# Two layers of cached attention and FFN for one token: w_down's rows and a head's keys laid adjacent per partition

## The chip, the cores and the metric

The kernel runs on one core of a Trainium2 chip. The metric is the device time of one execution in microseconds; the number for a kernel is the median over its runs. A profiled execution of its own gives the page and the trace; it has its own time and its own span (from the first to the last instruction).

## The reference

Four sequences (B = 4) each bring one token of 512 values. Two layers are run, and both use the same weights and the same caches, so every key and value is needed twice.

```
def attention(x):                       # Hq = 32 heads, Hkv = 8, Sk = 4096, Dh = 128
    q = x @ wq                          # [4, 512] @ [512, 4096]
    k, v = k_cache, v_cache             # [4, 8, 4096, 128] bf16, one kv head for 4 q heads
    p = softmax(q . k * Dh ** -0.5)
    return (p . v) @ wo                 # [4, 4096] @ [4096, 512]

def ffn(x):                             # F = 1792
    return (gelu(x @ w_gate) * (x @ w_up)) @ w_down

for layer in (1, 2):
    x = x + attention(layernorm(x))
    x = x + ffn(layernorm(x))
```

Keys and values are 33.5 MB each; w_gate, w_up and w_down are 1.8 MB each. The order in which the 4096 keys of a head are gone through doesn't matter, as long as keys and values use the same one. The same holds for the 1792 columns between w_gate, w_up and w_down.

## The kernel before

The partitions of SBUF are P = 128. A head's 4096 keys are split into NT = 2 tiles of 2048; a tile holds CH = 16 keys in each partition, 4 KB, and is loaded by one DMA of 512 KB (`cache_tile`; `load_pairs` loads the tiles of two heads by one DMA of 1 MB; `pump_head` loads both tiles of one head by one DMA of 1 MB, three times, for the last values). Before the change tile t of a head is its keys 2048 t to 2048 t + 2047, and partition p of it holds 16 neighbouring keys, so the whole tile is one stretch of 512 KB in memory.

All loads go through SP's queue (`dq`), in the order in which the code issues them; SP waits where the buffer of a load is still in use. Keys have one set of buffers (`KP`, 8 heads by 2 tiles). Values have a ring of eight buffers (`V_SLOTS`), which `VRing.pump` fills whenever one comes free.

The work goes sequence by sequence. The first layer's attention of sequence 0 runs alone (`attend_first`), and then, for each b:

- `dense(b, ...)`: the first layer's FFN of sequence b.
- the second layer's queries for b, its scores on the keys that lie in SBUF, and its values;
- `attend(b + 1, ...)`: as soon as the second layer's scores of b have read a key buffer, the keys of sequence b + 1 are loaded into it, turned in place on VectorE (`Keys.turn`, L484) and used for the first layer. Values of both are taken from the ring by `Values.step` and `Streamed.fill`.

After b = 3 (`attend_last`), `dense_last` computes the second layer's FFN for all four sequences at once.

The FFN is written in two ways. `ffn_in` (L374) has the weights as the stationary operand: for each of KF = 14 blocks c of 128 columns, and each of KD = 4 blocks k of 512 inputs, 128 x 128 weights are loaded and 32 columns are streamed past them: 56 weight loads and 56 matmuls. It is used for g and u of the first FFN (b = 0) and for u of `dense_last`. In the first FFN a few matmuls of no use are put in by `busy` (L435). `streamed` (L260, by way of `ffn_rows`) has the weights as the moving operand: the 1792 columns are cut into QD = 4 parts j, each of 14 x 32 columns, whose matmuls write to four groups of 32 partitions, side by side in TensorE; 4 x 4 matmuls of 448 columns, halfway through which `Streamed.fill` takes a value tile. A 32 x 32 transpose on VectorE (`turn_rows`, L277) then brings the result to partitions. This is used for g and u of the FFNs with b = 1, 2, 3, and, as `gate_rows` (L1083), for g of `dense_last`. `streamed` also serves the queries (`q_rows`) and the product with w_down (`down_rows`).

In all of them the result has the form [partition p, column c], c = 0 to 13, and before the change stands for the FFN's column 128 c + p, since `load_rest` lays row 128 c + p of w_down in partition p, place c. w_down is loaded in three parts, c from 0 to 5, 6 to 10 and 11 to 13 (`WD_PARTS`); each of its rows is 1 KB in memory.

`OutProj` (L319, through `mac`, L246) multiplies the attention's result with wo, the weights stationary, and a vector of one column, repeated 32 times by a step of 0, as the moving operand; for the last head of a sequence the vector is there four times (`OL_bf`), so that four adjacent elements are read.

Of the kernel before, what the change touches and what calls it, by code (L numbers as in the profile page):

```python
# [15 lines left out]
P = 128  # L16
# [3 lines left out]
QD = 4  # L20
QS = P // QD
# [13 lines left out]
def kernel(  # L35
# [19 lines left out]
    F = B_w_gate.shape[1]  # L55
    assert B == RUN and Sq == 1 and Dh == P and rep == QD and Hkv % GH == 0
    KD = D // P
    KF = F // P
    C = Sk // P
    NT = C // CH  # L60
# [29 lines left out]
    wg_sb = wts.tile([P, KD, F], BF16, name="wg_sb")  # L90
# [9 lines left out]
    xb = state.tile([P, KD, 2 * RUN], BF16, name="xb")  # L100
# [18 lines left out]
    def acc(shape, name):  # L119
        t = ps_ac.tile([P, 512], FP32, name=name, tag="acc")  # L120
        n = 1
        for s in shape:
            n *= s
        if len(shape) == 1:
            return t[:, :n]
        return t[:, :n].rearrange("p (a b) -> p a b", b=shape[1])

    def wide(v):
        n = v.shape[-1]
        return v.unsqueeze(1).broadcast_to([P, WIDE // n, n])  # L130

    def cache_tile(cache, b, kvh, t):
        return cache[b, kvh].rearrange("(t p c) d -> t p c d", t=NT, p=P)[t]

    def load_wq(g):
        n = HG * Dh
# [2 lines left out]
    def load_rest():  # L139
        n = Hq // 4  # L140
        for i in range(4):
            dq.dma_start(out=wo_sb[:, i * n:(i + 1) * n], in_=wo_dram[:, i * n:(i + 1) * n])
        dq.dma_start(out=wg_sb[:], in_=B_w_gate.rearrange("(k p) n -> p k n", p=P))
        dq.dma_start(out=wu_sb[:], in_=B_w_up.rearrange("(k p) n -> p k n", p=P))
        wd_dram = B_w_down.rearrange("(k p) n -> p k n", p=P)
        for lo, hi in zip(WD_PARTS, WD_PARTS[1:]):
            dq.dma_start(out=wd_sb[:, lo:hi], in_=wd_dram[:, lo:hi])

# [96 lines left out]
    def mac(dst, lhsT, rhs, first, last):  # L245
        nc.tensor.matmul(dst, lhsT=lhsT, rhs=rhs, start=first, stop=last, skip_group_check=True)  # L246
# [10 lines left out]
                    rhs(k) if nb > 1 else wide(rhs(k)), k == 0, k == KD - 1)  # L257
        return q

    def streamed(name, n, steps, halfway=None):  # L260


        full = acc([n, WIDE], name)
        flat = full.rearrange("p c r -> p (c r)")
        for i, (x, w) in enumerate(steps):
            if halfway and i == len(steps) // 2:
                halfway()
            blocks = w.rearrange("p (c j n) -> p j c n", j=QD, n=QS)
            for j in range(QD):
                nc.tensor.matmul(flat[j * QS:(j + 1) * QS], lhsT=x.broadcast_to([P, WIDE]),  # L270
                                 rhs=blocks[:, j], start=i == 0, stop=i == len(steps) - 1,
                                 skip_group_check=True)
        return full
# [10 lines left out]
                                        for k in range(KD)])  # L284

    def ffn_rows(b, w_sb, name, halfway):
        return streamed(name, KF, [(xb[:, k, b:b + 1], w_sb[:, k]) for k in range(KD)], halfway)

    def down_rows(H_bf):
        return streamed("y2", KD, [(H_bf[:, c, :1], wd_sb[:, c]) for c in range(KF)])  # L290
# [83 lines left out]
    def ffn_in(rhs, w_sb, name, halfway):  # L374
        g = acc([KF, WIDE], name)
        for c in range(KF):
            if c == KF // 2:
                halfway()
            for k in range(KD):
                mac(g[:, c], w_sb[:, k, c * P:(c + 1) * P], wide(rhs(k)), k == 0, k == KD - 1)  # L380
        return g

    def shifts(scr, mr, i):
# [69 lines left out]
    class Keys:  # L453
# [16 lines left out]
        def load_pairs(self, count, into=None):  # L470
            for _ in range(count):
                kvh, t = self.tile(self.nl)
                self.nl += 2
                to = into or KP[kvh // GH][t][kvh % GH // 2]
                pair = A_k_cache[self.b, kvh:kvh + 2].rearrange("h (t p c) d -> t p h c d",
                                                                t=NT, p=P)
                dq.dma_start(out=to[:], in_=pair[t])

# [117 lines left out]
    class VRing:  # L596
# [18 lines left out]
        def pump_head(self, pair):  # L615
            (layer, b, kvh, t), other = self.seq[self.at:self.at + 2]
            assert t == 0 and other == (layer, b, kvh, 1)
            self.at += 2
            dq.dma_start(out=pair,
                         in_=A_v_cache[b, kvh].rearrange("(t p c) d -> p t c d", t=NT, p=P))  # L620
            for t in range(NT):
                self.ready[(layer, b, kvh, t)] = (pair[:, t], False)

# [456 lines left out]
    def dense_last(y, full):  # L1080
        rows_g = full.rearrange("p c r -> p (c r)")

        def gate_rows():  # L1083
            for k in range(KD):
                blocks = wg_sb[:, k].rearrange("p (c j n) -> p j c n", j=QD, n=QS)
                for j in range(QD):
                    nc.tensor.matmul(rows_g[j * QS:j * QS + B], lhsT=xb[:, k, :B],
                                     rhs=blocks[:, j], start=k == 0, stop=k == KD - 1,
                                     skip_group_check=True)
            nc.vector.transpose(out=rows_g, in_=rows_g)  # L1090
            return full[:, :, :B]
# [8 lines left out]
        t = [apart(wq_sb[0], shape, i) for i in range(2)]  # L1100
# [16 lines left out]
        def rhs(k):  # L1117
            return xb[:, k, :RUN]

        g = gate_rows()  # L1120
# [26 lines left out]
        for k in range(KD):  # L1147
            (nc.sync, nc.scalar)[k % 2].dma_start(out=rows_out[:, k * P:(k + 1) * P],
                                                  in_=xo[k * QS:k * QS + B, :])
# [82 lines left out]
```

## Time and profile before

| | us |
|---|---|
| median of 3 runs | 281.35 |
| the three runs | 280.5, 281.35, 284.41 |
| the profiled execution | 278.11 |
| its span | 276.3 |
| busy in it: TensorE matmuls / weight loads | 175.1 / 117.7 |
| busy in it: VectorE / ScalarE | 173.6 / 48.6 |

SP's queue moved 104.08 MB in 32656 packets, which took 94.2% of what sixteen DMA engines have in the span. Of the packets 5888 are of 1 KB (wo and w_down), 1024 of 3.5 KB (w_gate, w_up) and nearly all others of 4 KB. TensorE's mean granted clock is 0.858.

In the page's slices each digit is the busy share of one fortieth of the span (6.9 us) in tenths. In a timeline each line begins with the start in us and the busy time of the instructions put together in it, and ends with the idle time before them and what ended it. In the chain of waits each line is a start, a duration and what was on the chain. Matmuls overlap, and the end of one is modelled: of a group of n, the last one's own duration is taken off to get at the pace of the others.

### The profile page before, as it was taken

Reading aid. Unit: us, or ns where it says so; the run is one execution under the profiler, and the core shown is the slowest. Engines: PE = TensorE matmul, PEld = TensorE weight load, DVE = VectorE, ACT = ScalarE, POOL = GpSimd, SP = SyncE. Lnnn points to the kernel's source line nnn. Section 1 sums busy time; section 2 is a strip of 40 time slices with the busy share of each in tenths; the row PEclk is TensorE's granted clock in tenths of the full one; section 3 lists DMA queues with packets and bytes.
Section 4 is the critical chain, followed back from the end, with each engine's and each line's share of the span. In section 5 each row is a group of like instructions: output and inputs, shape, how many; then the busy total and the mean of one; then the engine's idle time right before and its main releaser. Section 6 shows DMA issues by size and latency. Waiting matters only on the chain.

```text
span 276.3 us, 9468 instructions
## 1 busy us (share of the span) xinstructions
PE 175.1 (63%) x4240; PEld 117.7 (43%) x4243; DVE 173.6 (63%) x441; ACT 48.6 (18%) x107; POOL 2.7 (1%) x8
## 2 busy tenths in 40 slices
PE   1365163733877665777673548686738387967784
PEld 0313142633554524445453335464426154645573
DVE  3494942031236799766847898658677995576753
ACT  1001001000007202021312020311321203004340
POOL 2000000000000000000000000000000000000001
PEclk9999999555599986879996886899986777799999
DMA  6999999999967999999999999999999999999910
GB/s 254 420 419 419 416 423 416 402 385 410 400 246 252 416 416 420 416 417 419 409 342 419 416 418 418 415 410 411 336 417 419 417 419 416 422 400 407 417 56 3
DMA packets 32720, 104.69 MB, mean 379 GB/s; under 512 B 2724, under 2 KB 8616, under 8 KB 32680
## 3 DMA queue, kind: packets, MB, share of 16 engines
q1 hardware_dynamic: 32656, 104.08, 94.2%
q8 instruction: 33, 0.54, 0.7%
q14 instruction: 7, 0.06, 0.0%
q10 hardware_dynamic: 24, 0.01, 0.0%
HBM read 104.08 MB, written 0.00 MB: 377 GB/s over the span
## 4 chain that ended last, share of the span: by engine, by line
DVE 29%; PE 20%; DMA 10%; ACT 4%; issue 4%; DVEq 0%; SPq 0%; ACTq 0%
DVE kp L484 14%; DMA v_t<-in_A_v_cache_dram 6%; DMA kp<-in_A_k_cache_dram 5%; PE sc L515 4%; PE so L658 3%; PE ot L720 3%; PE x L561 2%; PE yr L347 2%; DVE pe L524 2%; DVE pe L542 1%; DVE so L666 1%; ACT pe L564 1%; PE y L246 1%; DVE qb L309 1%; DVE q L277 1%
## 5 line engine op out<-in xcount | busy, mean ns | idle before, releaser
L484 DVE STREAM_TRANSPOSE kp<-kp 128x1024 f32<-128x1024 f32 x64 | 74.8, 1212 | 3.7 <-DMA kp<-in_A_k_cache_dram 3.7
L515 PE MATMUL sc<-kp,qb 128*32 128x512 bf16 x512 | 48.2, 437 | 17.1 <-DVE kp L484 9.7
L720 PE MATMUL ot<-pe,v_t 128*128 128x32 bf16 x1120 | 34.2, 184 | 13.0 <-DMA v_t<-in_A_v_cache_dram 10.2
L720 PEld LDWEIGHTS <-v_t 128*128 128x128 bf16 x1120 | 32.3, 102 | 20.8 <-DMA v_t<-in_A_v_cache_dram 12.3
L515 PEld LDWEIGHTS <-qb 128*32 128x32 bf16 x512 | 15.5, 100 | 38.7 <-issue 22.6
L534 ACT ACTIVATE pe<-sc,nl 128x512 bf16<-128x512 f32 x8 | 5.5, 687 | 86.4 <-DVE pe L531 58.0
L561 PE MATMUL x<-pe,ident_bf 128*32 128x128 bf16 x192 | 6.4, 257 | 19.1 <-DVE pe L542 19.1
L246 PE MATMUL q<-xb,wq_sb 128*128 128x32 bf16 (+1 forms) x448 | 12.5, 174 | 5.6 <-DMA wq_sb<-in_A_wq_dram 5.6
L561 PEld LDWEIGHTS <-ident_bf 128*32 128x32 bf16 x256 | 5.8, 108 | 23.7 <-issue 21.9
L246 PEld LDWEIGHTS <-wq_sb 128*128 128x128 bf16 x448 | 11.9, 98 | 8.4 <-DMA wq_sb<-in_A_wq_dram 6.6
L524 DVE TENSOR_REDUCE pe<-sc 128x1 f32<-128x512 f32 x12 | 8.3, 691 | 10.6 <-PE sc L515 10.5
L666 DVE STREAM_TRANSPOSE so<-so 128x256 f32<-128x256 f32 (+1 forms) x19 | 11.1, 585 | 6.0 <-PE so L658 6.0
L547 PE MATMUL den<-zx,masks 128*128 128x16 f32 x32 | 8.4, 340 | 10.1 <-DVE qb L309 10.1
L246 PEld LDWEIGHTS <-wo_sb 128*128 128x128 bf16 x288 | 9.5, 101 | 9.2 <-DMA wo_sb<-in_A_wo_dram 7.2
L246 PE MATMUL y<-OT_bf,wo_sb 128*128 128x32 bf16 x224 | 8.1, 188 | 7.7 <-DMA wo_sb<-in_A_wo_dram 6.8
L658 PE MATMUL so<-v_t,pl 128*32 128x256 bf16 x192 | 9.6, 275 | 4.4 <-DMA v_t<-in_A_v_cache_dram 4.4
L594 DVE TENSOR_TENSOR OT_bf<-ot,rden 128x8 bf16<-128x8 f32 (+1 forms) x20 | 3.0, 150 | 14.9 <-PE ot L720 14.9
L547 PEld LDWEIGHTS den<-zx,masks 128*128 128x128 f32 x32 | 6.8, 263 | 12.6 <-issue 10.3
L658 PE MATMUL so<-v_t,pe 128*32 128x256 bf16 x208 | 11.0, 348 | 1.2 <-ACT pe L564 1.1
L366 DVE TENSOR_TENSOR xb<-XX,y 128x4 bf16<-128x4 f32 (+1 forms) x9 | 1.6, 174 | 14.7 <-PE y L246 14.6
L347 PE MATMUL yr<-wo_sb,OT_bf 128*2 128x512 bf16 (+1 forms) x88 | 10.5, 542 | 0.0
L542 DVE STREAM_TRANSPOSE pe<-pe 128x512 bf16<-128x512 bf16 x12 | 8.4, 697 | 3.4 <-ACT pe L534 3.4
(142 smaller groups left out, 206.7 us busy)
## 6 DMA issues: line engine op xcount, KB each, us to landing
v_t<-in_A_v_cache_dram SPq DMA_DIRECT2D x100, 512.0 KB, 7.7
kp<-in_A_k_cache_dram SPq DMA_DIRECT2D x40, 512.0 KB, 11.3
kp<-in_A_k_cache_dram SPq DMA_DIRECT2D x12, 1024.0 KB, 9.9
wq_sb<-in_A_wq_dram SPq DMA_DIRECT2D x2, 2048.0 KB
wo_sb<-in_A_wo_dram SPq DMA_DIRECT2D x4, 1024.0 KB, 11.2
wq_sb<-in_A_v_cache_dram SPq DMA_DIRECT2D x2, 1024.0 KB, 10.4
wg_sb<-in_B_w_gate_dram SPq DMA_DIRECT2D x1, 1792.0 KB, 12.3
wu_sb<-in_B_w_up_dram SPq DMA_DIRECT2D x1, 1792.0 KB
```

The source lines that it names most:

```text
L246: nc.tensor.matmul(dst, lhsT=lhsT, rhs=rhs, start=first, stop=last, skip_group_check=True)
L347: nc.tensor.matmul(self.rows[j:j + x.shape[1]], lhsT=x, rhs=wo_sb[:, i], start=self.n < QD, stop=True, skip_group_check=True)
L484: nc.vector.transpose(out=words, in_=words)
L515: nc.tensor.matmul(sc[s * QS:(s + 1) * QS], lhsT=qb[:, w0:w0 + 2 * W], rhs=kt[:, :, be // 2, :, be % 2], start=(t == 0 and be == 0), stop= ...
L524: nc.vector.tensor_reduce(out=m, in_=sc.rearrange("p c j -> p (c j)"), axis=AX.X, op=ALU.min if norm else ALU.max)
L534: nc.scalar.activation(out=pp[:], in_=sc[:], func=ACT.Exp, bias=nm, scale=norm.down if norm else scale, accum_out=ls)
L542: nc.vector.transpose(out=flat, in_=flat)
L547: nc.tensor.matmul(den[:], lhsT=mean_f[:, 0:1].broadcast_to([P, P]), rhs=zx[:], start=True, stop=True)
L561: nc.tensor.matmul(x[a * QS:(a + 1) * QS, s], lhsT=ident_bf[:, s * QS:(s + 1) * QS], rhs=pT[:, a], start=True, stop=True, skip_group_check ...
L658: nc.tensor.matmul(ps[d, :NW * QS], lhsT=x[:, w:w + NW].rearrange("p c h -> p (c h)"), rhs=v[:, i:i + NW, d], start=first and i == 0, stop ...
L666: nc.vector.transpose(out=flat, in_=flat)
L720: nc.tensor.matmul(self.ot[:, s % 2], lhsT=v[:, i, :], rhs=wide(pe[:, s, t * CH + i, :]), start=(done == 0 and i == 0), stop=(done == NT - ...
```

## The change

Four places read or write another order:

- `cache_tile`, `load_pairs` and `pump_head`: partition p now holds the 32 neighbouring keys 32 p to 32 p + 31, the first 16 in tile 0 and the rest in tile 1. A tile's piece per partition is 4 KB as before, but 8 KB from the next partition's; a whole head (`pump_head`) is one piece of 8 KB per partition. The same is done to keys and values.
- `load_rest`: partition p, place c of `wd_sb` holds row 14 p + c of w_down. The three parts are pieces of 6, 5 and 3 KB per partition in place of 1 KB each.
- `ffn_in` takes the columns c, c + 14, c + 28 ... of w_gate or w_up as its 128 stationary columns, with a step of 14 elements (28 bytes), where it took 128 adjacent ones.
- `ffn_rows` and `gate_rows` go through a part's 448 columns in the order that a step of 14 elements for the 32 columns of a block and a step of 1 from block to block give (`row_blocks` with `apart=True`), where the 32 columns were adjacent and the blocks 128 apart. `q_rows` and `down_rows` read as before.

```diff
     def cache_tile(cache, b, kvh, t):
-        return cache[b, kvh].rearrange("(t p c) d -> t p c d", t=NT, p=P)[t]
+        return cache[b, kvh].rearrange("(p t c) d -> t p c d", t=NT, p=P)[t]
...
-        wd_dram = B_w_down.rearrange("(k p) n -> p k n", p=P)
+        wd_dram = B_w_down.rearrange("(p k) n -> p k n", p=P)
...
+    def row_blocks(w, apart=False):
+        return w.rearrange("p (j n c) -> p j c n" if apart else "p (c j n) -> p j c n",
+                           j=QD, n=QS)
+
-    def streamed(name, n, steps, halfway=None):
+    def streamed(name, n, steps, halfway=None, apart=False):
...
-            blocks = w.rearrange("p (c j n) -> p j c n", j=QD, n=QS)
+            blocks = row_blocks(w, apart)
...
     def ffn_rows(b, w_sb, name, halfway):
-        return streamed(name, KF, [(xb[:, k, b:b + 1], w_sb[:, k]) for k in range(KD)], halfway)
+        return streamed(name, KF, [(xb[:, k, b:b + 1], w_sb[:, k]) for k in range(KD)], halfway,
+                        apart=True)
...
             for k in range(KD):
-                mac(g[:, c], w_sb[:, k, c * P:(c + 1) * P], wide(rhs(k)), k == 0, k == KD - 1)
+                mac(g[:, c], w_sb[:, k, c:F:KF], wide(rhs(k)), k == 0, k == KD - 1)
...
-                pair = A_k_cache[self.b, kvh:kvh + 2].rearrange("h (t p c) d -> t p h c d",
+                pair = A_k_cache[self.b, kvh:kvh + 2].rearrange("h (p t c) d -> t p h c d",
                                                                 t=NT, p=P)
...
             dq.dma_start(out=pair,
-                         in_=A_v_cache[b, kvh].rearrange("(t p c) d -> p t c d", t=NT, p=P))
+                         in_=A_v_cache[b, kvh].rearrange("(p t c) d -> p t c d", t=NT, p=P))
...
         def gate_rows():
             for k in range(KD):
-                blocks = wg_sb[:, k].rearrange("p (c j n) -> p j c n", j=QD, n=QS)
+                blocks = row_blocks(wg_sb[:, k], apart=True)
```

## The prediction

> **What bounds the kernel now.** I read the page's forty slices first, then the windows around the dip in them, then the timeline of the first feed-forward (FFN) stage, the chain of waits, and last the timeline of the last stage.
>
> ```profile
> DMA  6999999999967999999999999999999999999910
> GB/s 254 420 419 419 416 423 416 402 385 410 400 246 252 416 416 420 416 417 419 409 342 419 416 418 418 415 410 411 336 417 419 417 419 416 422 400 407 417 56 3
> ```
>
> The queues move about 418 GB/s nearly all the time, so 104 MB fill some 249 us of the 276. What is left is the start, the end (hardly anything is loaded after 264 us), one hole at 80 to 86 us and two dents at 138 and 195 us. A change pays or costs where it moves these.
>
> ```profile
> 69.89 1.68 PE L246 MATMUL g<-xb,wg_sb 128*128 128x32 bf16 x56 [2.78 <-DMA wg_sb<-in_B_w_gate_dram]
> 71.78 2.34 PE L439 MATMUL idle<-wg_sb,ident_bf 128*128 128x512 bf16 x5 [0.22 <-issue]
> 74.25 1.51 PEld L246 LDWEIGHTS <-wu_sb 128*128 128x128 bf16 x56 [1.04 <-DMA wu_sb<-in_B_w_up_dram]
> 76.95 0.75 PE L246 MATMUL y<-words,wd_sb 128*128 128x32 bf16 x24 [0.21 <-DVE words L429]
> 79.53 0.17 DVE L366 TENSOR_TENSOR xb<-XX,y 128x4 bf16<-128x4 f32 x1 [2.72 <-PE y L246]
> 83.96 1.91 SPq L477 DMA_DIRECT2D kp<-in_A_k_cache_dram  x3
> ```
>
> These lines (timeline, first FFN, and SP's queue after it) tell why there is a hole. w_gate, w_up and w_down arrive just in time for their matmuls; their result goes through normalisation, queries and scores, and only when the scores have been read (SP at 83.96) may the next keys be loaded into those buffers. Whatever delays y at 79.5 widens the hole by the same amount. DMA and PE are nearly level here: PE has its idle matmuls done at 74.1, w_up is there at 74.25; `words` (the FFN's hidden vector H) is ready at 76.95, the first part of w_down at 76.92.
>
> ```profile
> 130.19 0.40 PE so L658 x8
> 130.59 0.40 PE u L270 x8
> 131.02 0.68 DVE u L277
> ...
> 138.08 6.50 DMA kp<-in_A_k_cache_dram
> ```
>
> The chain of waits at the second FFN (the third is alike): a value tile lands at 130.19, then the second half of u is streamed, turned, and so on to 138.08, where SP may load keys again, with the dent behind it. So the eight matmuls of u's second half lie on the path. After 201.8 us no DMA stands in the chain; the fourth FFN and the last stage are compute only:
>
> ```profile
> 268.97 0.93 PE L1087 MATMUL gr<-wg_sb,xb 128*4 128x448 bf16 x16
> 269.83 1.56 PE L246 MATMUL u<-xb,wu_sb 128*128 128x32 bf16 x56
> 271.44 0.21 DVE L1137 TENSOR_TENSOR wq_sb<-u,wq_sb 128x56 f32<-128x56 f32 x1 [0.24 <-PE u L246]
> ```
>
> **The change part by part.** No instruction and no wait is added or taken; pieces and strides change.
>
> *w_down's load.* 1792 pieces of 1 KB become 384 of 3 to 6 KB. The windows give 386 GB/s while wo's 1 KB pieces pass (56 to 63 us) and 419 with 4 KB pieces (30 to 44), over 16 engines 42.4 and 156 ns a piece: some 4 ns per piece beside 38 ns per KB. 1408 pieces fewer on 16 engines are 0.36 us. What is late next is `words`, already level with w_down's first part. The later parts cost waits of 0.30 and 0.43 us before PE's weight loads, but the idle matmuls queued there fill most of that: 2.5 us of PE work from 76.95 end at 79.45 against the 79.5 seen. I take 0.1 us gained at best, and nothing once `words` is later. SP's three issues of w_down (61.55 to 72.1) get shorter and the first key pair behind them on its queue is issued sooner, but it lands behind the same bytes, and the other three wait for the scores.
>
> *Whole heads of the last values.* Three loads of 1 MB (SP, 249.5 to 252.4) go from 4 to 8 KB pieces: 384 pieces fewer, 4 ns each over 16 engines, 0.1 us. No DMA is in the chain there, so nothing. Without that cover it is 0.1 us gained.
>
> *All other keys and values.* Pieces stay at 4 KB, but lie 8 KB apart in memory instead of adjacent. wq's loads have had that shape all along (half of an 8 KB row): the window 16.7 to 21.7, mostly wq, shows 421 GB/s, and 4 to 9, wq first and then keys, 426; the contiguous tiles show 416 to 419. I take nothing; a loss and a gain are rivals below.
>
> *The weights of the FFN.* Here is the cost. H's element in partition p and column c must now be row 14p+c of w_down, so gate and up are no longer read as adjacent columns but as every 14th, 28 bytes apart: as the moving operand in L270 and L1087 (448 columns, four matmuls side by side), as the stationary one in `ffn_in` (56 weight loads of 128 columns). No row of the trace reads at 28 bytes, so bounds. Now: the sixteen of L1087 take 0.93 us, the last alone 0.35, so three quads pass in 0.58, 0.19 us each (0.43 ns a column). Lower bound: the same; the scores (L515) read at 4 bytes' step and lose little. Upper bound from the same row: 32 in 1.99 us at 137 us, the last 0.39, so 0.229 us a quad of 512 columns, in which the read moves on by 16 bytes every four columns, 1.8 ns for each such move; if every 28-byte step cost that, a quad takes 0.81 us. Between them stands the row of OutProj (timeline at 124.6): a vector read one element at a time, sixteen matmuls of 32 columns in 0.66 us, against 0.55 at 126.0 where four adjacent elements are read. Less the last one's 0.19 and 0.18, that is 31 against 25 ns each: 1 ns per element read singly. It is the nearest row (single elements, the same engine), so I take 1 ns: a quad takes 0.45 us, eight matmuls 0.90 for 0.38, sixteen 1.04 us more, and a weight load (32 columns at a time, as 128 in 25 ns show that several are read at once) 32 ns for 25 at clock 1.0 and for 27 at 0.5.
>
> The Trainium skill, page "Advanced Engine Details and Errata", section "SBUF Cachelines", speaks against this change: SBUF has lines of 16 bytes, and at least two hits on a line are needed to absorb its latency. Taken as half speed, an estimate by that page is 0.38 us a quad and +2.8 us in all; no run here shows such a stride. The page "TensorE: Matmul & The Clock Gate", section "Weight-path perf modes", says that the fast weight load takes strided columns too; this trace shows only packed ones.
>
> *Where it lands.* First FFN: g 56 x 5 ns = 0.3, of which 0.1 is covered by w_up's landing; u 56 x 7 = 0.4: y is 0.5 us later (the 0.1 of w_down is gone). Second FFN: g's first half fills PE to 127.93, its second to 129.04 instead of about 128.24; gate's DVE chain (2.3 us from its turn) ends at 131.6 and holds up u's turn, which u itself would reach at 131.54: +0.6. Third, the same sum: the values' landing at 187.55 covers u's first half, gate's chain ends 0.7 after u's turn of before: +0.7. Fourth: less waiting for values, both halves of g pass on, +1.0. Each of the three moves the keys' loads, or the end, by as much. Last stage: L1087 +1.04 and u 56 x 6.5 ns = +0.36, one after the other on PE: +1.4. Sum: 0.5 + 2.3 + 1.4 = 4.2, say 4 us. On the profiled execution: 278.11 (span 276.3) + 4 = 282.1. That execution lies 3.2 under the median of the three runs, 281.35, so I say 285.4 for the median, own range 283.5 to 287.
>
> **The rivals.**
>
> *Slower than 2%: the steps cost 1.8 ns, not 1.* Place: the four quads of every g and u. Then eight matmuls take 1.61 us, and the four halves with three value tiles between them 7.1: they no longer fit between landings, and u ends 3.3, 3.3 and 3.9 us later in the three FFNs. A weight load takes 58 ns: 3.4 us in the first FFN, and 2.5 + 1.8 in the last stage. Sum 18: 299.5. It decides from 1.1 ns a column on, where the sum passes 5.6 us; 1.4 ns gives 11 (292). For it: the scores' quads are 0.229 and not 0.213 us, as if such moves were already the limit. Against it: the row read singly. 0.33.
>
> *The stride is free.* The four-byte row points there. 281.3. 0.10.
>
> *Keys and values 8 KB apart load worse.* At the rate of the 1 KB pieces, 386, the 72 MB of 85.6 to 262.5 us take 14 us longer: with the 4 above, some 299. wq speaks against it. 0.07.
>
> *Faster by over 2%:* loads at 426 throughout would save about 3.3 us of those 72 MB; with a free stride as well that is 278, and more than that no row offers. 0.03.
>
> **The numbers.** The forecast has 0.47: 285.4. Low end 281, the free stride; high end 297, most of the first rival, which leaves out its top and the loads' rival, less than 2 in 10. 2% is 5.6 us and about what a measurement tells from no change (the three runs span 3.9). Faster 0.03, within 2% 0.57 (forecast and free stride), slower 0.40.
>
> **What would show it.** L1087's sixteen at 1.97 us (0.45 a quad): 0.93 means a free stride, over 2.2 the first rival. u's weight loads in the last stage: 56 in 1.9 us. y of the first FFN 0.5 us later against w_up's landing, and the hole as much wider. Windows with keys alone at 416 to 421 GB/s; below 410 the loads are the cause. w_down in 4.4 us instead of 4.8, with no wait before its second and third part. I am wrong if PE reads at a stride much better or worse than singly, or if the fast weight load fails at a stride.

## The result, and the profile after

| | before | after |
|---|---|---|
| median, us | 282.12 (4 runs, 280.5 to 284.41) | 309.57 (4 runs, 306.31 to 310.63) |
| after / before, 95% interval | | 1.1006 (1.0943 to 1.1069) |
| the profiled execution: time / span | 278.11 / 276.3 | 309.21 / 307.4 |
| busy TensorE matmuls / weight loads | 175.1 / 117.7 | 202.8 / 127.2 |
| mean granted clock | 0.858 | 0.817 |

The kernel is 27.5 us slower, above the range of the prediction (281 to 297). The two profiled executions differ by 31.1 us, since the one of before lies 4 under its median and the one of after at its own. Some runs of the kernels below fell into a slower state, a longer time at a lower clock; the medians are over all runs, the ratios over the others.

First the page's slices of the kernel after (one fortieth of its span is 7.7 us):

```profile
DMA  7999999999529999998799999987999999889200
GB/s 268 368 417 420 417 421 415 382 403 422 209 63 346 415 419 417 417 380 280 229 398 420 409 417 418 406 288 229 360 414 416 419 416 419 288 276 415 99 2 3
```

Where values stream without a break the rate is as before, 414 to 421 GB/s. But the hole of the first FFN is deeper (209 and 63 GB/s against 246 and 252), the dents of the second and third FFN are 280, 229 and 288, 229 against single slices of 342 and 336, a third dent (288, 276) stands at the fourth, and the second slice has 368 for 420. So there are two things: loads that start later, and loads that run slower while the DMA digit still says 9.

The timeline of the first FFN after (start, busy time; L246 is the matmul of `mac`, L482 the load of key pairs):

```profile
71.31 3.44 PEld L246 LDWEIGHTS <-wg_sb 128*128 128x128 bf16 x56 [2.83 <-DMA wg_sb<-in_B_w_gate_dram]
...
77.21 3.52 PE L246 MATMUL u<-xb,wu_sb 128*128 128x32 bf16 x56
...
82.24 0.81 PE L246 MATMUL y<-words,wd_sb 128*128 128x32 bf16 x24
...
84.75 0.17 DVE L371 TENSOR_TENSOR xb<-XX,y 128x4 bf16<-128x4 f32 x1 [3.08 <-PE y L246]
...
89.12 1.74 SPq L482 DMA_DIRECT2D kp<-in_A_k_cache_dram  x3
```

56 weight loads take 3.44 us where they took 1.6: 60 ns each for 27. TensorE waits for w_gate once, and from then on it is itself the limit: w_up is there when it is wanted, y starts as soon as `words` is there, and no part of w_down is waited for. The keys' loads (89.12, before 83.96) move by as much as y does (84.75, before 79.53). The chain of waits at the second FFN shows the other form (start, duration; L274 is the strided stream, L281 the turn; the dots between the four streams are value tiles of 0.2 to 0.4 us):

```profile
135.18 1.71 PE g L274 x7
...
137.30 1.61 PE g L274 x7
...
139.14 1.61 PE u L274 x6
...
140.97 1.65 PE u L274 x8
142.64 0.68 DVE u L281
...
149.69 7.69 DMA kp<-in_A_k_cache_dram
```

All four halves stand in it end to end, 1.61 to 1.71 us each; before, only the last half was on the path, with 0.40. The last stage, from its timeline:

```profile
294.89 3.42 PE L1092 MATMUL gr<-wg_sb,xb 128*4 128x448 bf16 x16
...
298.24 3.55 PE L246 MATMUL u<-xb,wu_sb 128*128 128x32 bf16 x56
...
302.66 1.66 PE L1132 MATMUL yo<-wd_sb,wq_sb 128*4 128x128 bf16 x56 [0.45 <-DVE wq_sb L1145]
```

Against 0.93, 1.56 and, for the last line's 56 matmuls on adjacent weights, 0.95 us.

To place the difference I cut each trace at the residual additions (the starts of `xb<-XX,y`; L371 above is one) and took the length of each piece. The columns give the pieces of before and what is added to them in one profiled execution of each kernel; the last four kernels are the experiments below.

| piece, us | before | after | ffn_only | kv_only | adjacent_longer | pairs_only |
|---|---|---|---|---|---|---|
| start and first attention | 66.6 | +1.5 | -0.1 | +1.0 | -0.2 | +0.1 |
| FFN, b = 0 | 12.9 | +3.8 | +4.0 | -0.1 | +3.7 | 0.0 |
| attentions | 47.1 | +2.6 | -0.1 | +1.4 | +0.2 | +2.6 |
| FFN, b = 1 | 7.0 | +3.8 | +3.4 | +0.7 | +3.0 | +0.7 |
| attentions | 50.3 | +1.5 | +0.6 | +3.9 | +0.9 | +1.2 |
| FFN, b = 2 | 7.1 | +3.3 | +3.7 | +0.6 | +2.9 | +0.4 |
| attentions | 50.2 | +1.9 | -0.5 | +1.9 | 0.0 | +0.7 |
| FFN, b = 3 | 6.7 | +3.9 | +3.9 | +0.4 | +4.5 | +0.8 |
| last attention | 20.4 | +3.7 | +0.5 | +0.3 | +0.3 | 0.0 |
| last stage | 8.1 | +5.2 | +5.2 | 0.0 | +4.5 | 0.0 |

After: 20.0 in the FFNs and the last stage, 11.2 outside them.

### The profile page after: what moved, and what is told of

It is laid out like the page before. It is cut to its first block, busy times and chain, and to the rows that moved or that the text cites. A ratio compares the mean times of both kernels' runs of the same rounds, so it can differ in the third digit from the quotient of the medians.

```text
span 307.4 us, 9471 instructions
## 1 busy us (share of the span) xinstructions
PE 202.8 (66%) x4243; PEld 127.2 (41%) x4243; DVE 174.3 (57%) x441; ACT 48.7 (16%) x107; POOL 2.7 (1%) x8
## 4 chain that ended last, share of the span: by engine, by line
PE 24%; DMA 22%; DVE 18%; issue 2%; ACT 2%; DVEq 0%; SPq 0%; ACTq 0%
DMA v_t<-in_A_v_cache_dram 17%; DVE kp L489 9%; DMA kp<-in_A_k_cache_dram 5%; PE ot L725 4%; PE sc L520 3%; PE g L274 3%; PE u L274 3%; PE so L663 2%; PE y L246 1%; PE u L246 1%; DVE so L671 1%; PE gr L1092 1%; PE x L566 1%; DVE q L281 1%; ACT pl L539 1%
## 5 line engine op out<-in xcount | busy, mean ns | idle before, releaser
L725 PE MATMUL ot<-pe,v_t 128*128 128x32 bf16 x1120 | 36.1, 185 | 17.5 <-DMA v_t<-in_A_v_cache_dram 14.3
L725 PEld LDWEIGHTS <-v_t 128*128 128x128 bf16 x1120 | 33.1, 102 | 27.3 <-DMA v_t<-in_A_v_cache_dram 19.3
L552 PE MATMUL den<-zx,masks 128*128 128x16 f32 x32 | 8.8, 353 | 12.9 <-DVE qb L314 12.9
L246 PE MATMUL q<-xb,wq_sb 128*128 128x32 bf16 (+1 forms) x448 | 12.6, 174 | 6.1 <-DMA wq_sb<-in_A_wq_dram 6.1
L246 PEld LDWEIGHTS <-wq_sb 128*128 128x128 bf16 x448 | 11.9, 98 | 8.9 <-DMA wq_sb<-in_A_wq_dram 7.1
L663 PEld LDWEIGHTS <-pl 128*32 128x32 bf16 x240 | 6.7, 106 | 16.7 <-issue 16.0
L246 PE MATMUL y<-OT_bf,wo_sb 128*128 128x32 bf16 x224 | 8.1, 188 | 7.6 <-DMA wo_sb<-in_A_wo_dram 7.1
L246 PEld LDWEIGHTS <-wo_sb 128*128 128x128 bf16 x288 | 9.4, 102 | 8.9 <-DMA wo_sb<-in_A_wo_dram 7.6
L274 PE MATMUL u<-wu_sb,xb 128*32 128x448 bf16 x48 | 10.8, 979 | 0.0
L274 PE MATMUL g<-wg_sb,xb 128*32 128x448 bf16 x48 | 10.8, 982 | 0.0
```

The lines of the kernel that those rows point to most:

```text
L552: nc.tensor.matmul(den[:], lhsT=mean_f[:, 0:1].broadcast_to([P, P]), rhs=zx[:], start=True, stop=True)
L663: nc.tensor.matmul(ps[d, :NW * QS], lhsT=x[:, w:w + NW].rearrange("p c h -> p (c h)"), rhs=v[:, i:i + NW, d], start=first and i == 0, stop ...
L725: nc.tensor.matmul(self.ot[:, s % 2], lhsT=v[:, i, :], rhs=wide(pe[:, s, t * CH + i, :]), start=(done == 0 and i == 0), stop=(done == NT - ...
```

## The experiments

**One half of the change alone.** `ffn_only` is the kernel after with the three loads of keys and values as before; `kv_only` is the kernel before with only these three changed.

```diff
-        return cache[b, kvh].rearrange("(t p c) d -> t p c d", t=NT, p=P)[t]
+        return cache[b, kvh].rearrange("(p t c) d -> t p c d", t=NT, p=P)[t]
...
-                pair = A_k_cache[self.b, kvh:kvh + 2].rearrange("h (t p c) d -> t p h c d",
+                pair = A_k_cache[self.b, kvh:kvh + 2].rearrange("h (p t c) d -> t p h c d",
...
-                         in_=A_v_cache[b, kvh].rearrange("(t p c) d -> p t c d", t=NT, p=P))
+                         in_=A_v_cache[b, kvh].rearrange("(p t c) d -> p t c d", t=NT, p=P))
```

(This is `kv_only`; `ffn_only` has all the other hunks of the change.)

> Only the other part: w_down by 3 to 6 KB and gate and up read at a step of 28 bytes; keys and values as before. Theory A: 306 to 310 us, ratio 1.09 to 1.105, the attention stretches between the FFNs longer by the same 1.5 to 2.6 us as in the changed kernel. Rival B: 297 to 301 us, attention stretches as before the change.

> Only the keys' and values' order of the change (4 KB pieces 8 KB apart, whole heads by 8 KB); w_down, gate and up as before. Theory A (all of the loss comes from the strided reads of gate and up on TensorE, and from the value loads that wait behind them): 280 to 284 us, ratio 0.995 to 1.01, windows with keys and values alone at 416 to 421 GB/s. Rival B (the loads' order costs the part of the loss that lies outside the FFNs, some 9 to 11 of 31 us of span): 289 to 293 us, ratio about 1.03.

Measured: `ffn_only` 299.67 us against 279.55, ratio 1.0722 (1.0624 to 1.0819); `kv_only` 287.22 against the same 279.55, ratio 1.0254 (1.0179 to 1.0328). 20.1 and 7.7 us make 27.8, the whole is 27.5: the two halves add up. `ffn_only` is where rival B put it, with the attentions as before; `kv_only` lies above theory A's range and below B's 289 to 293, so B had the cause and overrated its size. The table above puts all of the first into the FFNs and the last stage, and nothing of it into the attentions; most of the second lies outside the FFNs. In `kv_only` nothing on any compute engine is changed, and its slices show where it goes:

```profile
DMA  6999999999939999999999999999999999999920
GB/s 265 364 417 421 416 421 418 396 387 416 395 137 307 405 416 421 417 413 392 322 378 390 414 421 354 370 381 326 344 342 416 418 416 417 420 390 370 417 94 3
```

364, 354, 370, 381, 326, 344, 342 under a 9: the queues are busy and move less. The packets of 4 KB take 159 ns in the median, as ever; at 136 to 146, 172 to 177 and 182 to 215 us 7 to 12 in a hundred take over 250, in `before` five in its own dent (138 to 146) and one in the whole. Not all of it is shown to belong to the change: the stretches at 172 to 178 and 182 to 188 us (343 and 336 GB/s) lie in the midst of the values' stream, where `after` has 416 (165 to 195 us) and `keys_only` and `values_only`, both below, 411 to 417. They are in one execution, which is 10 us longer than the profiled one of before, where the medians differ by 7.7.

**What a stride costs TensorE.** `steps_probe` is the kernel before with a row of matmuls at its end that no output uses: 16 matmuls of 448 columns (four side by side) with the moving operand read at steps of 1 to 16 elements, then 16 weight loads of 128 columns at seven steps.

```diff
+        for s, word in ((1, "one"), (2, "two"), (3, "three"), (4, "four"), (5, "five"), (6, "six"), (7, "seven"), (8, "eight"), (10, "ten"), (12, "twelve"), (14, "fourteen"), (16, "sixteen")):
+            t = ps_sc.tile([P, 512], FP32, name=f"step_{word}", tag="sc")
+            for r in range(16):
+                j = r % QD * QS
+                nc.tensor.matmul(t[j:j + QS, :448], lhsT=xb[:, 0, :1].broadcast_to([P, WIDE]),
+                                 rhs=flat_w[:, 0:448 * s:s], start=True, stop=True,
+                                 skip_group_check=True)
...
+                mac(t[:, :WIDE], flat_w[:, 0:P * s:s], wide(xb[:, 0, :RUN]), True, True)
```

> The kernel before, and after its last store a row of tests: sixteen matmuls (four quads) of 448 columns at steps of 1, 2, 3, 4, 5, 6, 7, 8, 10, 12, 14 and 16 elements, then sixteen weight loads of 128 columns at steps of 1, 2, 4, 7, 8, 14 and 16. Line theory (each move into another 16 bytes costs 1.77 ns, so a step of s elements costs s/8 of that until 8): quads of 0.19, 0.20, 0.30, 0.40, 0.50, 0.59, 0.69, 0.79 us and then no more. Rival (a step function at 16 bytes): 0.19 up to a step of 7, 0.79 from 8 on. Second rival (any element not adjacent to the last is read singly): 0.79 from a step of 3 on. Weight loads: 25 ns to 60 ns in the same form.

TensorE's timeline of it, sixteen matmuls to a line:

```profile
273.99 0.93 PE L1156 MATMUL step_one<-wg_sb,xb 128*32 128x448 bf16 x16
274.75 0.98 PE L1156 MATMUL step_two<-wg_sb,xb 128*32 128x448 bf16 x16
...
276.74 1.82 PE L1156 MATMUL step_four<-wg_sb,xb 128*32 128x448 bf16 x16
...
285.47 3.43 PE L1156 MATMUL step_eight<-wg_sb,xb 128*32 128x448 bf16 x16
...
295.05 3.56 PE L1156 MATMUL step_fourteen<-wg_sb,xb 128*32 128x448 bf16 x16
...
301.75 0.56 PE L246 MATMUL held_one<-xb,wg_sb 128*128 128x32 bf16 x16
...
304.93 1.12 PE L246 MATMUL held_fourteen<-xb,wg_sb 128*128 128x32 bf16 x16
```

By the starts in the trace, at a granted clock of 1.00, a quad of matmuls takes (medians): step 1 0.189 us, 2 0.199, 3 0.297, 4 0.400, 5 0.495, 6 0.594, 7 0.691, 8 0.787, and 0.79 to 0.81 from there to 16. This is a straight line through zero, 99 ns per unit of step, cut off below by 0.189 and bent flat at a step of 8 elements, 16 bytes, as the line theory has it; steps 3 to 7 contradict both rivals. In other words, each move of the read to another 16 bytes costs 1.77 ns; of adjacent columns eight share one, at step 2 four, at step 4 two, from step 8 on each column has its own. A matmul alone needs 0.42 ns a column, so four columns to a line are enough to hide it and two are not. The weight load follows nearly the same line, as if four columns were read at a time (28, 50 and 57 ns by it at steps 4, 7 and 8): 25 ns at steps 1 and 2, 33 at 4, 53 at 7, 60 to 62 from 8 on.

**Is it only TensorE's time?** `adjacent_longer` is the kernel before, weights adjacent and w_down as before, in which every quad of g and u is followed by three more (`more` is 3 there) on a stationary operand of zeros, and every weight load by one or two more: TensorE is kept as long, at steps of one.

```diff
+            for j in range(more * QD):
+                j = j % QD
+                nc.tensor.matmul(flat[j * QS:(j + 1) * QS],
+                                 lhsT=qb[:, 0:1].broadcast_to([P, WIDE]),
+                                 rhs=blocks[:, j], start=False, stop=i == len(steps) - 1,
+                                 skip_group_check=True)
...
+                for _ in range(1 + k % 2):
+                    mac(g[:, c], w_sb[:, k, c * P:(c + 1) * P],
+                        wide(qb[:, 0:rhs(k).shape[1]]), False, k == KD - 1)
```

> The kernel before, its columns read adjacent, but TensorE kept as long in gate and up as in the changed kernel: each quad of 448 columns is streamed three more times with a stationary operand of zeros (4 x 0.19 = 0.76 us a quad against 0.79), each weight load of the stationary form gets one or two more (2.5 x 25 = 62 ns against 60). Theory A1 (only TensorE's time in the FFNs counts, wherever it comes from): 303 to 311 us. Rival C (the strided reads cost something beside their own time, by a lower granted clock or by slowing others): 296 to 302 us, with the granted clock near 0.86 instead of 0.82.

Measured: 299.57 us, ratio 1.0684 (1.0613 to 1.0754), against 299.67 of `ffn_only`. The time lies in rival C's range and not in A1's, but both ranges were set against the whole change, and keys and values are as before here. Against `ffn_only`, the half that it copies, the whole is the same, and the pieces of the FFNs and the last stage differ by 0.3 to 0.8 us, four of them shorter here and one longer. So TensorE's time in the FFNs, wherever it comes from, is enough to make the loss; slower loads, or other engines held up by the strided reads, are not needed for it. In the last stage (4.5 for 5.2 us) the difference is the clock: the 56 matmuls on w_down take 0.95 us at a granted clock of 1.00 here, as before the change, and 1.66 at 0.50 in the kernel after and in `ffn_only`. Why the clock is lower there isn't shown.

**A smaller step.** `pairs_of_columns` lays w_down by pairs of rows, 2 KB per piece, so that gate and up are read at a step of 2 elements; keys and values as before.

```diff
-        wd_dram = B_w_down.rearrange("(k p) n -> p k n", p=P)
+        wd_dram = B_w_down.rearrange("(g p e) n -> p g e n", p=P, e=2)
...
-            blocks = w.rearrange("p (c j n) -> p j c n", j=QD, n=QS)
+            blocks = row_blocks(w, paired)
...
+            return w.rearrange("p (g j n e) -> p j g e n", j=QD, n=QS, e=2)
...
+                mac(g[:, c], w_sb[:, k, (c // 2) * 2 * P + c % 2:(c // 2 + 1) * 2 * P:2], wide(rhs(k)), k == 0, k == KD - 1)
```

> The kernel before with another order of w_down alone: two neighbouring rows adjacent in a partition, pieces of 2 KB (parts of 6, 4 and 4 columns), and gate and up read at a step of 2 elements, which the row of tests showed at 0.20 us a quad against 0.19 and 25 ns a weight load. Theory A: 279 to 280.5 us, no change that can be measured (0.2 us of loads less, 0.1 us of TensorE more). Rival (any step costs the FFNs' path): 284 us or more.

Measured: 281.53 us against 281.45, ratio 1.0022 (0.998 to 1.0063). The step of 2 costs nothing that can be measured, as the probe has it; and pieces of 2 KB in place of 1 KB in w_down gain nothing either.

**Which loads of keys and values?** `keys_only` has the new order in the keys' loads alone:

```diff
-                dq.dma_start(out=k_tile(kvh, t), in_=cache_tile(A_k_cache, self.b, kvh, t))
+                dq.dma_start(out=k_tile(kvh, t), in_=A_k_cache[self.b, kvh].rearrange("(p t c) d -> t p c d", t=NT, p=P)[t])
...
-                pair = A_k_cache[self.b, kvh:kvh + 2].rearrange("h (t p c) d -> t p h c d",
+                pair = A_k_cache[self.b, kvh:kvh + 2].rearrange("h (p t c) d -> t p h c d",
```

`runs_of_32k` is another layout of keys and values altogether: groups of eight partitions hold 32 KB in one stretch, and the two tiles of a head alternate by such stretches; pairs and heads are loaded tile by tile.

```diff
-        return cache[b, kvh].rearrange("(t p c) d -> t p c d", t=NT, p=P)[t]
+        return cache[b, kvh].rearrange("(q t r c) d -> t q r (c d)", t=NT, q=16, r=8)[t]
```

> Only the keys are loaded by pieces 8 KB apart, the values adjacent as before, so that keys and values of a head are in different orders and the output is another one; time alone is meant. If each load of the new order loses by itself: keys are 33 of the 87 MB of caches that are loaded, so 282 to 283 us. If the loss comes from keys and values in the new order meeting in the queue: 279 to 281 us. If it is the keys: 285 to 287 us.

> The kernel before with keys and values in a third order: eight partitions' pieces adjacent (32 KB), then a gap of 32 KB that holds the other half; pairs and whole heads are loaded tile by tile. If the loss of the kernel with only the keys' and values' order changed (287.2 us, ratio 1.025) comes from the small distance of 8 KB between single pieces: 279 to 281.5 us. If any tile that is not one stretch of 512 KB loses (the same memory stretched over 1 MB): 285 to 288 us.

`keys_only`: 286.34 us against 281.45, ratio 1.0178 (1.0123 to 1.0233); +4.9 us for 33.5 MB, so the cost doesn't go by bytes. `runs_of_32k`: 403.51 us, ratio 1.4302 (1.4198 to 1.4406), at 250 to 280 GB/s in most slices. It was a poor test: the sixteen DMA engines were busy all the time (a share of 1.03 at 266 GB/s from 30 to 60 us), and a 4 KB packet took 240 ns in the median, for 159 before. But the shape of the source, 16 by 8 instead of 128, changed together with where the pieces lie, so the run doesn't tell which of the two made the packets slow.

**The loads by themselves.** `loads_probe` is the kernel before with long streams of loads behind it, no compute alongside: 24 tiles each in five orders, then eight whole heads by 8 KB, then wq.

```diff
+        stream(adjacent, halves)
+        stream(apart_8k, halves)
+        stream(apart_8k, firsts)
+        stream(adjacent, mixed)
+        stream(apart_8k, mixed)
+        for i in range(8):
+            dq.dma_start(out=KP[i // 4][i // 2 % 2][i % 2][:],
+                         in_=A_v_cache[3, i].rearrange("(p t c) d -> p t c d", t=NT, p=P))
+        for i in range(4):
+            load_wq(i % 2)
```

> The kernel before, and after its last store nothing but loads, back to back on SP's queue: 24 tiles of values with adjacent pieces, the same 24 with pieces 8 KB apart (both halves of a head in turn), 24 first halves 8 KB apart, 24 tiles of keys and values in turn with adjacent pieces, the same 8 KB apart, 8 whole heads by 8 KB pieces, wq four times. Theory P (pieces 8 KB apart load slower by themselves): 416 to 421 GB/s for adjacent pieces, 360 to 400 for pieces 8 KB apart, 420 to 428 for whole heads. Rival Q (a steady stream is not slower; only in the kernel, after gaps or beside waiting loads, do such pieces get in each other's way): 414 to 421 in all of them, wq 421.

Windows in the midst of four of the streams: adjacent, 8 KB apart, keys and values in turn 8 KB apart, whole heads (the last column is GB/s, the one before it the DMA share):

```profile
285.00:300.00 15.00, 0.00 (x0) 0.00 (x0) 0.00 (x0) 0.00 (x0) 0.00 (x0) 0.50 1.03 420
312.00:330.00 18.00, 0.00 (x0) 0.00 (x0) 0.00 (x0) 0.00 (x0) 0.00 (x0) 0.50 1.03 420
...
400.00:420.00 20.00, 0.00 (x0) 0.00 (x0) 0.00 (x0) 0.00 (x0) 0.00 (x0) 0.50 1.03 418
430.00:440.00 10.00, 0.00 (x0) 0.00 (x0) 0.00 (x0) 0.00 (x0) 0.00 (x0) 0.50 1.01 428
```

A steady stream of pieces 8 KB apart is not slower. So the 8 KB by themselves fell as the cause, and what was left was something in how the kernel loads: beside compute, in its own order, or after a break.

`loads_beside` puts these behind the kernel before, each in both orders:

```diff
+        for _ in range(80):
+            turned(slots[0][:], 1)
+        idle.clear()
+        busy(320)
+        stream(apart_8k, key_units(32))
+        stream(adjacent, key_units(32))
+        for order in (apart_8k, adjacent):
+            one_by_one(order, key_units(12))
...
+        for order in (apart_8k, adjacent):
+            pause()
+            start(order)
```

> Before, with loads alone at its end, all without use for the output: 32 key tiles 8 KB apart and then 32 adjacent ones beside VectorE transposes of 1.2 us and TensorE matmuls; then 12 tiles of each order one by one, each issued after the one before has landed; then 12 pairs of heads of each order; then, after a pause, the kernel's own first loads (half of wq, eight key tiles, the other half, eight key tiles) in each order. C, compute alongside is what makes the new order slow: the first 32 go at 340 to 390 GB/s, the adjacent 32 at 418, and all later sections are alike in both orders. G, an empty queue does (engines that start in step): one by one, a tile 8 KB apart takes over 5% longer from issue to landing than an adjacent one; streams alike. S, the order of the first keys does by itself: the start in the new order dips to 300 GB/s or less within its first 10 us, as at 8 to 10 us of the changed kernel, and the adjacent one doesn't. Pairs: if they are slow, under 400 against 419. If all sections are alike within 2%, what makes it slow is none of these and stays open.

C fell: beside VectorE at 97% and TensorE at 99% the stream 8 KB apart began at 328 and 379 GB/s, but then ran at 414 to 420 with the same compute alongside, as the adjacent one did (TensorE beside it up to 346 us). For S, the kernel's first loads are half of wq, eight key tiles, the other half, eight key tiles; three of the stretches of key tiles (9 us each) are the first eight in the new order, the second eight in the new order, and the first eight in the old:

```profile
529.00:538.00 9.00, 0.00 (x0) 0.00 (x0) 2.32 (x2) 0.00 (x0) 0.00 (x0) 0.50 1.00 379
545.00:554.00 9.00, 0.00 (x0) 0.00 (x0) 0.00 (x0) 0.00 (x0) 0.00 (x0) 0.50 1.03 420
563.00:572.00 9.00, 0.00 (x0) 0.00 (x0) 0.00 (x0) 0.00 (x0) 0.00 (x0) 0.50 1.03 420
```

A dip in the first eight, though not to 300 as S had it, and none in the second. The pause that was meant to stand before each start did not come about (a DMA share of 1.03 from 517 to 526 us), so this dip has no break before it, only wq. The twelve pairs went at 401 GB/s in the new order and at 421 in the old, again with the slow windows early. One by one, a tile 8 KB apart took, by its packets, some 1.7 us for a head of odd number and 2.3 for one of even number, an adjacent tile 1.84 to 2.05: a mean of 1.99 against 1.92, 4%, short of G's 5%. All of the slow stretches lie early in their section, but the adjacent streams here followed others without a break, and so I gave each order the same beginning, several times:

> Before, with loads at its end that have no use for the output: sections of twelve key tiles (6.3 MB, 15.0 us at 419 GB/s), each section begun after all earlier loads have landed and a pause of some 7 us; four sections with adjacent tiles, four with tiles 8 KB apart, in turn; then two with pieces of 4 KB that lie 32 KB apart, and three each of six pairs of heads in both orders. G, after a pause the sixteen engines start in step, and in step the new order collides until they have drifted apart: the first 5 us of a section 8 KB apart stay under 390 GB/s where the adjacent ones reach 400 and more, and a section takes 0.8 to 1.5 us longer, in each of the four. Some six starts and holes at 1 us each would then be most of the 7.7 us of the order of keys and values. N, the slow beginnings of 8 KB streams seen so far (328, 379 and then 420 GB/s) were those of any stream: both orders take the same time within 0.3 us. If G holds through the pitch, 32 KB apart is slower still or alike; if it is at 419 at once, the pitch alone is not the reason.

```diff
+        def tiles(order, b):
+            pause(singles[0])
+            for i in range(12):
+                dq.dma_start(out=singles[i], in_=order(b, i))
+            for i in range(12):
+                pause(singles[i][:, :1])
...
+        for b in range(B):
+            for order in (adjacent, apart_8k):
+                tiles(order, b)
+        for b in range(2):
+            tiles(apart_32k, b)
+        for b in range(3):
+            for form in ("h (t p c) d -> t p h c d", "h (p t c) d -> t p h c d"):
+                pairs(form, b)
```

The first 9 us of some sections: adjacent tiles, 8 KB apart, 32 KB apart, pairs adjacent, pairs 8 KB apart:

```profile
284.90:293.90 9.00, 0.00 (x0) 0.00 (x0) 5.64 (x25) 0.00 (x0) 0.00 (x0) 0.50 1.00 376
314.60:323.60 9.00, 0.00 (x0) 0.00 (x0) 5.09 (x23) 0.00 (x0) 0.00 (x0) 0.50 0.98 332
...
526.70:535.70 9.00, 0.00 (x0) 0.00 (x0) 5.21 (x23) 0.00 (x0) 0.00 (x0) 0.50 1.02 382
...
643.10:652.10 9.00, 0.00 (x0) 0.00 (x0) 2.95 (x12) 0.00 (x0) 0.00 (x0) 0.50 1.00 382
670.00:679.00 9.00, 0.00 (x0) 0.00 (x0) 2.70 (x12) 0.00 (x0) 0.00 (x0) 0.50 0.92 349
```

All seven comparisons of neighbours go the same way: 376, 370, 358, 364 against 332, 335, 336, 326 for single tiles, 382, 382, 381 against 349, 349, 348 for pairs. G is half borne out. After a break the new order is slower for the first 9 us, by 0.3 MB or some 0.75 us of loading for single tiles; the first 5 us, of which G spoke, are slow in both orders (324 to 345 GB/s adjacent, 318 to 321 apart). With single tiles the loss hardly reaches the end of a section: 17.4 us in the mean adjacent, 17.7 apart, about what N has, since the adjacent sections end with a few late packets. With pairs it is more than G had: 16.25, 16.36 and 16.76 us adjacent, 19.21, 18.73 and 18.72 apart, 2.4 us in the mean. And pieces 32 KB apart (382 and 388 GB/s) are as fast as any, so the distance between pieces isn't the reason as such.

**The kernel again, with parts of the new order.** `pairs_only` changes the loads of key pairs alone, `values_only` those of the values:

```diff
-                pair = A_k_cache[self.b, kvh:kvh + 2].rearrange("h (t p c) d -> t p h c d",
+                pair = A_k_cache[self.b, kvh:kvh + 2].rearrange("h (p t c) d -> t p h c d",
```

```diff
-                dq.dma_start(out=v, in_=cache_tile(A_v_cache, *key[1:]))
+                dq.dma_start(out=v, in_=A_v_cache[key[1], key[2]].rearrange("(p t c) d -> t p c d", t=NT, p=P)[key[3]])
...
-                         in_=A_v_cache[b, kvh].rearrange("(t p c) d -> p t c d", t=NT, p=P))
+                         in_=A_v_cache[b, kvh].rearrange("(p t c) d -> p t c d", t=NT, p=P))
```

> Of the change only the order of the twelve loads of key pairs (load_pairs); all other keys and the values stay, so the keys are in mixed orders and the time alone is meant. All keys in the new order cost 4.9 us, of which the start of the trace held 0.9. After a pause six such pairs took 2.4 us longer than before, twelve single tiles 0.2 us. If the pairs behind the three holes carry the cost of the keys, as G has it, this one is slower by 3 to 6 us (ratio 1.01 to 1.02), in the three attentions after the first, with the first 85 us of the trace as before. If the cost comes with every key load in the new order (12.6 of the 33.5 MB are pairs), it is 1.8 us. If it comes with the single tiles, nothing (ratio 0.997 to 1.003).

> The values alone lie 8 KB apart (three whole heads by 8 KB pieces); the keys stay as before, so keys and values are in different orders and the time alone is meant. Keys alone cost 4.9 us, keys and values together 7.7. If a load in the new order is slower by a share of its own, the values, whose loads are more bytes than the keys', should cost at least what the keys did: 286 or more. If what matters is that loads follow each other in the order of the keys (four tiles t = 0, then four t = 1, after wq, and pairs), values cost little: 282 to 283, ratio under 1.01, with slice 1 of the page back at 420 GB/s (364 with keys and values). If the two add up, 281.5 + 2.8 = 284.

`pairs_only`: 285.45 us against 281.56, ratio 1.0119 (1.0052 to 1.0186), +3.3 us by the ratio, with the first 80 us as before. It is within what G says, and nearly twice what the bytes of the pairs would make; at the lower end of the interval, 1.5 us, the bytes can't be excluded. `values_only`: 282.07 against 280.36, ratio 1.0045 (1.0003 to 1.0086), +1.3 us for the larger part of the bytes, with its second slice at 421 GB/s. So the cost goes with the order of the keys: 3.3 for the twelve pairs behind the holes, 5.0 for all keys, of which the start's piece has 0.9; 1.3 for the values.

## Why the prediction was wrong, step by step

*The failed step: the 1 ns of a column.* I had two bounds for a 28-byte step, 0.19 and 0.81 us a quad, and chose 0.45 by "the nearest row", OutProj's vector read singly. A quad takes 0.79 to 0.81, a weight load 60 ns. The upper bound, worked out from the scores' row as 1.8 ns for each move by 16 bytes, was the price itself (1.77). OutProj's row has a single element, repeated by a step of 0: 32 reads of the same 16 bytes. Within a matmul the row has no move to another 16 bytes, which is what the change adds (what its own 1 ns is due to, no run took up); the scores' row, with a step of 4 bytes, does have it, and its 0.229 us is 128 such moves. The scores' row was near by mechanism, OutProj's only by look.

*What followed from it, by the first rival.* That rival gave +3.4 for the first FFN, +3.3, +3.3 and +3.9 for the others, 2.5 + 1.8 for the last stage. In `ffn_only` it is +4.0, +3.4, +3.7, +3.9 and 5.2. So the placing was right, with all four halves on the path because they no longer fit between landings; 18 us was said, 20.1 measured. Missing were 0.6 in the first FFN, 0.4 in the third and 0.9 in the last stage; of the last, 0.7 are the 56 matmuls on w_down, which I had left as they were and which ran at a granted clock of 0.50. It decided, as said, by the price of a column. The whole, 27.5, lies above my high end for a second reason: the rival of the column and the rival of the loads were priced each by itself, and both were at work.

*The page on SBUF's lines.* The Trainium skill, "Advanced Engine Details and Errata", section "SBUF Cachelines", has lines of 16 bytes and asks for at least two hits to absorb the latency. The line length agrees: the cost stops growing at a step of 16 bytes. Two hits are not enough here: at a step of 4 elements, two columns to a line, a quad takes 0.400 us for 0.189; four are (0.199). My estimate from that page, half speed, was too low by a factor of two. The other, "TensorE: Matmul & The Clock Gate", section "Weight-path perf modes", says the fast weight load takes strided columns. It seems so: 128 columns in 60 ns are nearly four times faster than a column per 1.77 ns.

*The second failed step: keys and values, "I take nothing".* It is 7.7 us by `kv_only`. The rows that I read, wq at 421 and 426 GB/s, were right of a steady stream, and `loads_probe` has the same 418 to 420. They didn't show what other loads of the same shape do early after the start or after a break. At the kernel's start it isn't the first load that is slow: wq is 8 KB apart there before and after, but from 8 to 11 us, with the first eight key tiles behind it, the kernels with keys in the new order have 291 (`after`), 296 (`kv_only`) and 303 GB/s (`keys_only`), `before` and `values_only` 418 and 419. The most of it is behind the holes, where the pairs are loaded: 3.3 us by `pairs_only`. The loads' rival, 14 us by a rate of 386 throughout, had the right cause and the wrong form: 290 to 350 GB/s for some 3 to 10 us after the start and the breaks, 416 in between. Why the new order is slow there stays open. That engines which start together hit the same part of memory would fit the long packets, the difference between even and odd heads, and the recovery, but not the dip behind wq without a break; the trace shows no addresses, and no run took that apart. The Trainium skill, "DMA: Bandwidth & Descriptors", section "Latency and other measured facts", tells of slow copies where the rows of the partitions lie 2 MiB and more apart, and infers streams in lock step. Both distances here lie far under its range, and of the two the wider is the faster, 382 and 388 against 326 to 336, which its direction doesn't lead one to expect.

*What was right.* w_down's larger pieces and whole heads gain nothing that can be seen: in the kernel after no matmul waits for w_down, and `pairs_of_columns` and `values_only` show no gain. Whole heads do go at 428 GB/s in `loads_probe`, but nothing on the path waits for the last three. The hole widens with y, as said: y is 5.2 us later, 1.5 of it from the first attention, and so are the keys' loads.

*What stays unexplained.* In the last attention the profile of after has 3.7 us more, neither half alone over 0.5; 2.04 of it is one stretch in the chain that the profile puts down to "issue" (at 279.16), time in which nothing that the profile shows was waited for. It is in one execution; the trace of before has such a stretch too, 1.35 us at 153.

No version tried was faster than the kernel before.

## What to carry to other kernels

A change of layout that is meant to help a load is paid by whoever reads the tile: count for each operand of TensorE how many of the elements in 16 bytes of SBUF are used in a row, and price a move to the next 16 bytes by a row that really makes such moves, not by one that looks alike. A rate read in the midst of a stream doesn't price a load that starts after a break, and another tensor's load of the same shape doesn't either; look for a row with these loads and a beginning in it. And where the moving operand of TensorE has to be strided, a step of two elements of bf16 costs next to nothing here, four doubles the time, eight and more quadruples it; a weight load takes 33 ns for 25 at four and 60 from eight on.

## What the runs showed of the hardware

- The 1.77 ns don't scale with the granted clock. Windows of the kernel after, in the halves of g at 135.2 and 137.3 (the third last column is the clock):

```profile
135.20:136.80 1.60, 1.60 (x12) 0.28 (x16) 0.80 (x5) 0.41 (x2) 0.00 (x0) 0.50 0.84 328
137.30:138.90 1.60, 1.60 (x17) 0.32 (x12) 0.00 (x0) 0.00 (x0) 0.00 (x0) 1.00 0.83 292
```

  Eight matmuls take 1.6 us at 0.50 and at 1.00; a strided stream is bound by its read.
- The mean granted clock doesn't single out strided reads: over four runs each it was 0.84 in `ffn_only`, 0.86 in `adjacent_longer`, and 0.83 in `kv_only`, which has none.
- In a steady stream pieces of 8 KB went at 428 GB/s and pieces of 4 KB at 418 to 420, adjacent or 8 KB apart (`loads_probe`).
- In `runs_of_32k`, with tiles read as 16 by 8 partitions from stretches of 32 KB, all engines were busy and loads went at 250 to 280 GB/s, a 4 KB packet in 240 ns.
